# A planner that orders five engines: measured durations, a latency per engine, a port shared by two engines, and a transfer queue

## The chip, the cores and the metric

The kernel runs on one core of a Trainium2 chip. Its engines run their own instruction streams: TensorE (PE, with its weight loads PEld), VectorE (DVE), ScalarE (ACT), GpSimd (POOL), and SyncE (SP), which here only issues transfers. The metric is the device time of one launch in microseconds (us).

## The reference

Two blocks in a row, in float32: attention over a sliding window of 64 positions, and an expert-like layer ("SoLU" with a layer norm).

```python
# q, k, v: (8, 8, 576, 64); q and k are scaled by 6.12 beforehand
scores = q @ k.transpose(0, 1, 3, 2) / 8
scores = where((rel >= 0) & (rel < 64), scores, -1e9)      # rel = query - key
attn = exp(scores - max) / (sum + 1e-9)
x = (attn @ v) as 4608 tokens of 512
h = x @ w_in                                               # 512 x 1024
e = exp(h - max(h));  solu = h * e / (sum(e) + 1e-9)
ln = (solu - mean(solu)) / sqrt(var(solu) + 1e-6) * g_ln
out = ln @ w_out                                           # 1024 x 512
```

The weights w_in, w_out come as float64 and are brought to float32 on the chip by bit operations.

## The kernel before

The 4608 tokens are 36 tiles of 128. For each tile t the program does, in this order:

- **scores** (L375, PE): queries by keys into the PSUM tile pS. DVE (L390) takes the negative maximum of each of 8 heads (nmx) and moves the scores to SBUF (sS); ACT (L395) does the exponentials and their sums (sm); DVE (L408, L411) turns the sums into reciprocals (rec); POOL (L413) multiplies, one instruction for each head, 8 a tile.
- **transposes of the probabilities**: for tiles 0 to 4 on PE (L448) and copied to PT (L453). From tile 5 on ACT packs them by halves into a tile "raw" (L427), a transposing transfer on SP turns each half (L430), and DVE copies it to PT (L437), two copies a tile.
- **values** (L472, PE): V by PT into pO; ACT and DVE split the result into a high part xH (L486) and a rest xL (L487).
- **first matrix** (L515, PE): 24 matmuls of 128x512, three for each product (xH by the high weights, xH by their rest w, xL by the high weights) into pH. pH has one buffer of two banks: the next tile's L515 can't start before this tile's pH has been read.
- **norm**: DVE takes the maximum (L530, to a column of mst), ACT the exponential e (L532), DVE the product e·h and its sum (L535, the last reader of pH), then small columns on DVE (L538 to L546), ACT squares (L541), POOL takes the power −1/2 (L548), DVE a last product (L549), and POOL scales the two halves of e (L552).
- **transposes of e**: DVE packs each half (L578), a transfer turns it (L581), DVE unpacks it to y (L591), ACT and DVE split it into yH (L595) and yL (L597). The first three and last two tiles go through PE (L612).
- **second matrix** (L648, PE): 24 matmuls into pO, copied by ACT (L655) and stored by SP (L656).

The stages of several tiles overlap: scores run 3 or 4 tiles ahead of L515, and L648 two tiles behind it. From tile 6 on, tiles go in pairs: PE does the values of two tiles, the scores of two tiles, then L648, L515, L648, L515. In the first 66 us the weights are converted (L288 to L296) and split into a high part and a rest w (L312 to L319), and the first three tiles use plain float32 matmuls (L504, L636).

The order on each engine isn't written out. The code adds each piece of work to a `Plan` with an engine, a cost in ns, the tiles that it reads and writes, and a latency. `Plan.order` gives each piece a due time, counted back from the order in which PE's work was added, and then simulates the five engines: of the pieces that are ready on the engine that is free first, it takes the one due earliest. The instructions are emitted in the order that comes out, and on the chip each engine runs its own strictly in that order. SP is one of these engines, so a transfer that waits holds up those behind it. Pieces marked "loose" may leave the order in which they were added.

Of the kernel before, what the change touches and what calls it, by code (L numbers as in the profile page):

```python
# [57 lines left out]
class Plan:  # L58
# [4 lines left out]
    LATENCY = 150  # L63
# [6 lines left out]
    def op(self, engine, cost, emit, reads, writes, lat=0, loose=False):  # L70
        self.ops.append((engine, cost, emit, reads, writes, lat + self.LATENCY, loose))

    def dma(self, size, emit, reads, writes, loose=False):
        self.op("SP", max(350, size // (RATE if loose else 340)), emit, reads, writes, 2600, loose)

    def edges(self):
# [37 lines left out]
    def order(self):  # L114
# [31 lines left out]
        out = []  # L146
        while any(waiting.values()):
# [21 lines left out]
def tile_window_attention_solu_moe(  # L169
# [92 lines left out]
    def weight_block(i, src):  # L262
# [20 lines left out]
        for x in parts:  # L283
# [7 lines left out]
                tf()[:, x], tf()[:, x], EXP_LO, EXP_HI, ALU.max, ALU.min), [W], [W])  # L291
            plan.op("DVE", n // 3 * 2 + 18, lambda x=x: nc.vector.tensor_scalar(
                t()[:, x], t()[:, x], 0x07FFFFFF, 3, ALU.bitwise_and, ALU.logical_shift_left), [W], [W])
            plan.op("DVE", n + 170, lambda x=x: nc.vector.scalar_tensor_tensor(
                t()[:, x], hi()[:, x], -0x40000000, t()[:, x], ALU.bitwise_and, ALU.bitwise_or), [R, W], [W])
# [10 lines left out]
    def split(i):  # L306

        for x in range(2):
            reads = [("w", i), ("w", i, x), ("w", NC + 1 if i < NC else NW - 1)]
            last = reads[:2] + [("H", i, x)], [("w", NW + i, x)]  # L310
            if i < NC:
                plan.op("ACT", 600, lambda x=x: nc.scalar.copy(WH(i, x), W32(i)[:, x]), reads, [("H", i, x)])  # L312
                plan.op("DVE", 620, lambda x=x: nc.vector.tensor_sub(  # L313
                    WL(i)[:, x], W32(i)[:, x], WH(i, x).bitcast(F32)), *last)
# [4 lines left out]
            plan.op("DVE", 620, lambda x=x, f=f: nc.vector.scalar_tensor_tensor(  # L319
                WL(i)[:, x], W32(i)[:, x], g_sb[:, f:f + 1], WH(i, x).bitcast(F32), ALU.mult, ALU.subtract), *last)  # L320
# [39 lines left out]
    def scores(t):  # L360
# [22 lines left out]
    def softmax(t):
# [4 lines left out]
        for h in range(H):  # L388

            plan.op("DVE", 215, lambda h=h: nc.vector.tensor_tensor_reduce(  # L390
                SS(t)[:, h], PS(t)[:, h % 2, h // 2], mk, scale=-SCALE, scalar=BIG,
                op0=ALU.add, op1=ALU.min, accum_out=cols("nmx", h)),
                [("pS", t, h // 4)], [("sS", t, h), ("nmx", t, h)], lat=300)
        for h in range(H):
# [3 lines left out]
                [("nmx", t, h)], [("sS", t, h), ("sm", t, h)], lat=400)  # L398
# [6 lines left out]
        for o in range(0, H, n):  # L405
            s = slice(o, o + n)
            R = ("rec", t, o)
            plan.op("DVE", 160, lambda s=s: nc.vector.tensor_scalar_add(  # L408
                rec()[:, s], T("sm", t, [P, H], pool=st)[:, s], 1e-9),
                [("sm", t, h) for h in range(o, o + n)], [R])  # L410
            plan.op("DVE", 160, lambda s=s: nc.vector.reciprocal(rec()[:, s], rec()[:, s]), [], [R])  # L411
            for h in range(o, o + n):
                plan.op(engine, cost, lambda h=h: v.tensor_scalar(  # L413
                    SS(t)[:, h], SS(t)[:, h], rec()[:, h:h + 1], 0.0, ALU.mult, ALU.add),
                    [R], [("sS", t, h)])
# [18 lines left out]
    def transposes(t):
        if t >= CROSS_P:
            for x in range(2):
# [3 lines left out]
                    [("raw", NW + 2 * t, 2 + x)], [("PT", t, x)])  # L440
# [248 lines left out]
    def group(t):  # L689
        on(values, t + 1)  # L690
        if t != PAIRS:
            on(values, t + 2)
# [107 lines left out]
```

## Time and profile before

| | us |
|---|---|
| median of 3 runs (530.92 to 532.55) | 532.03 |
| the profiled execution | 531.16 |
| its span, first to last instruction | 529.4 |
| PE busy | 504.7 |
| DVE busy | 417.3 |
| ACT busy | 356.0 |
| POOL busy | 224.6 |

The granted TensorE clock is 0.999 over the span. PE's own records are pipelined: a matmul of 128x512 lasts 0.40 us in the records, while the next one starts after about 0.235. So a run of matmuls without gaps is recognised by the starts, not by the records' lengths. Of the transfers, SP issues 36 loads of queries and keys (qk, 640 KB), 36 of v (512 KB), 36 stores (256 KB) and 124 transposes; from issue to landing they take 5.3, 4.8, 2.7 and 3.2 us in the median.

### The profile page before, as it was taken

How to read it: one execution, taken by the hardware profiler on the slowest of the kernel's cores; microseconds unless marked ns; L12 is line 12 of the kernel's file. 1: busy time of each engine (PE TensorE's matmuls, PEld its weight loads, DVE VectorE, ACT ScalarE, POOL GpSimd, SP SyncE). 2: the span in 40 equal slices, each digit the busy share in tenths (PEclk: the TensorE clock that was granted, in tenths of full speed). 3: DMA queues.
4: the chain of work that ended last, by engine and by line, in shares of the span. 5: the costliest groups of instructions: out<-in, count | busy, mean ns of one | idle time of the engine just before them, and what ended most of it. 6: DMA issues, size and time to landing. Idle time of an engine off the chain costs nothing.

```text
span 529.4 us, 11654 instructions
## 1 busy us (share of the span) xinstructions
PE 504.7 (95%) x4072; PEld 392.2 (74%) x4072; DVE 417.3 (79%) x1327; ACT 356.0 (67%) x959; POOL 224.6 (42%) x406
## 2 busy tenths in 40 slices
PE   2779999999999999999999999999999999999996
PEld 2345577787888887787878787888788878787774
DVE  4979999888797878696978787978787878796631
ACT  4588776669586767777676768585858585855331
POOL 2056066444625460626261727272727272713220
PEclk9999999999999999999999999999999999999999
DMA  8994226887959798777789696969796959555201
GB/s 319 409 399 146 89 85 114 185 198 172 216 134 170 209 183 198 150 229 150 230 147 232 138 241 130 249 132 247 132 248 127 250 120 213 111 129 115 65 21 40
DMA packets 148507, 93.57 MB, mean 177 GB/s; under 512 B 132960, under 2 KB 132960, under 8 KB 148064
## 3 DMA queue, kind: packets, MB, share of 16 engines
q1 hardware_dynamic: 148448, 92.83, 72.1%
q8 instruction: 32, 0.52, 0.4%
q14 instruction: 27, 0.22, 0.1%
HBM read 50.86 MB, written 9.44 MB: 114 GB/s over the span
## 4 chain that ended last, share of the span: by engine, by line
PE 58%; DVE 17%; POOL 8%; DMA 8%; ACT 6%; issue 2%; ACTq 0%; POOLq 0%; DVEq 0%
PE pH L515 23%; PE pO L648 19%; DMA raw<-raw 7%; POOL sS L413 5%; PE pO L472 4%; PE pS L375 4%; PE pH L504 3%; DVE sS L390 3%; PE pO L636 3%; POOL e L552 3%; DVE y L591 3%; DVE e L535 2%; ACT sS L395 2%; DVE raw L578 2%; DVE mst L530 1%
## 5 line engine op out<-in xcount | busy, mean ns | idle before, releaser
L413 POOL TENSOR_SCALAR sS<-sS,rec 128x128 f32<-128x128 f32 x280 | 123.7, 460 | 50.7 <-DVE nmx L390 26.7
L395 ACT ACTIVATE sS<-sS,nmx 128x128 f32<-128x128 f32 x288 | 112.0, 392 | 10.5 <-DVE nmx L390 10.2
L648 PE MATMUL pO<-w_outH,yH 128*128 128x512 f32 x272 | 110.3, 405 | 0.0
L515 PE MATMUL pH<-w_inH,xH 128*128 128x512 f32 x264 | 106.3, 403 | 1.9 <-DVE mst L535 1.6
L648 PE MATMUL pO<-w,yH 128*128 128x512 f32 x272 | 108.1, 397 | 0.0
L548 POOL TENSOR_TENSOR mst<-mst,neghalf 128x1 f32<-128x1 f32 x36 | 28.2, 784 | 187.6 <-DVE mst L546 187.6
L648 PE MATMUL pO<-w_outH,yL 128*128 128x512 f32 x272 | 106.8, 393 | 0.0
L515 PE MATMUL pH<-w,xH 128*128 128x512 f32 x264 | 104.2, 398 | 0.0
L515 PE MATMUL pH<-w_inH,xL 128*128 128x512 f32 x264 | 103.6, 392 | 0.0
L552 POOL TENSOR_SCALAR e<-e,mst 128x512 f32<-128x512 f32 x72 | 69.5, 972 | 50.9 <-DVE mst L549 23.7
L427 ACT COPY raw<-sS 128x1024 uint16<-128x1024 uint16 x62 | 64.8, 1045 | 36.5 <-POOL sS L413 36.3
L515 PEld LDWEIGHTS pH<-w_inH,xH 128*128 128x128 f32 x264 | 49.5, 188 | 17.4 <-PE pO L648 4.3
L648 PEld LDWEIGHTS pO<-w_outH,yH 128*128 128x128 f32 x272 | 51.0, 187 | 15.0 <-issue 1.9
L648 PEld LDWEIGHTS pO<-w_outH,yL 128*128 128x128 f32 x272 | 51.1, 188 | 12.7
L541 ACT ACTIVATE sq<-e,mst 128x1024 bf16<-128x1024 f32 x36 | 41.4, 1151 | 27.1 <-DVE mst L538 22.7
L648 PEld LDWEIGHTS pO<-w,yH 128*128 128x128 f32 x272 | 51.1, 188 | 10.8
L530 DVE TENSOR_REDUCE mst<-pH 128x1 f32<-128x1024 f32 x36 | 43.8, 1216 | 19.5 <-PE pH L515 18.7
L578 DVE COPY raw<-e 128x1024 uint16<-128x1024 uint16 x62 | 45.2, 732 | 17.5 <-POOL e L552 17.5
L515 PEld LDWEIGHTS pH<-w_inH,xL 128*128 128x128 f32 x264 | 49.6, 188 | 12.6 <-DVE w L313 0.2
L515 PEld LDWEIGHTS pH<-w,xH 128*128 128x128 f32 x264 | 49.6, 188 | 11.3 <-issue 0.2
L591 DVE COPY y<-raw 128x1024 uint16<-128x1024 uint16 x62 | 48.6, 787 | 10.4 <-DMA raw<-raw 10.3
L390 DVE CUSTOM_DVE_ANT_0 sS<-pS,maskNone 128x128 f32<-128x128 f32 x224 | 53.5, 283 | 2.3 <-PE pS L375 1.9
(66 smaller groups left out, 743.6 us busy)
## 6 DMA issues: line engine op xcount, KB each, us to landing
qk<-qk SPq DMA_DIRECT2D x36, 640.0 KB, 5.3
v<-vS SPq DMA_DIRECT2D x36, 512.0 KB, 4.8
y<-ot SPq DMA_DIRECT2D x36, 256.0 KB, 2.7
raw<-w_out SPq DMA_DIRECT2D x4, 1024.0 KB, 11.8
raw<-w_in SPq DMA_DIRECT2D x3, 1024.0 KB, 11.9
raw<-raw SPq DMA_TRANSPOSE x124, 3.2
raw<-w_in SPq DMA_DIRECT2D x2, 512.0 KB, 6.6
g_sb<-gT SPq DMA_DIRECT2D x1, 4.0 KB, 14.3
```

Of the source, the lines that this page charges most:

```text
L390: plan.op("DVE", 215, lambda h=h: nc.vector.tensor_tensor_reduce(SS(t)[:, h], PS(t)[:, h % 2, h // 2], mk, scale=-SCALE, scalar=BIG, op0=A ...
L395: plan.op("ACT", 390, lambda h=h: nc.scalar.activation(SS(t)[:, h], SS(t)[:, h], AF.Exp, bias=cols("nmx", h), scale=-1.0, accum_out=cols(" ...
L413: plan.op(engine, cost, lambda h=h: v.tensor_scalar(SS(t)[:, h], SS(t)[:, h], rec()[:, h:h + 1], 0.0, ALU.mult, ALU.add), [R], [("sS", t, h)])
L427: plan.op("ACT", 1050, lambda x=x: nc.scalar.copy(XP(t)[:, x], SS(t)[:, 4 * x:4 * x + 4].bitcast(U16).rearrange("p h (n w) -> p w (h n)", ...
L515: plan.op("PE", 233, lambda n=n, c=c, x=x, w=w: nc.tensor.matmul(PH(t)[:, hs], x(t)[:, c], WH(c, h) if w is WH else WL(c)[:, h], start=(n ...
L530: plan.op("DVE", 1150, lambda: nc.vector.tensor_reduce(nmax(), PH(t), axis=AX.X, op=ALU.max, negate=True), [("pH", t)], [key(0)])
L541: plan.op("ACT", 1200, lambda: nc.scalar.activation(T("sq", t, [P, DFF], BF16), E(t), AF.Square, bias=nmean(), scale=1.0, accum_out=ss()), ...
L548: plan.op("POOL", 560, lambda: nc.gpsimd.tensor_tensor(kk(), kk(), neghalf, op=ALU.pow), [], [key(5)])
L552: plan.op("POOL", 770, lambda h=h, hs=hs: nc.gpsimd.tensor_scalar(E(t)[:, hs], E(t)[:, hs], nmean(), kk(), ALU.add, ALU.mult), [key(4), ke ...
L578: plan.op("DVE", 740, lambda h=h: nc.vector.tensor_copy(EP(t, h), E(t)[:, h * 512:(h + 1) * 512].bitcast(U16).rearrange("p (n w) -> p w n" ...
L591: plan.op("DVE", 740, lambda h=h: nc.vector.tensor_copy(Y(h).bitcast(U16).rearrange("p f (n w) -> p f w n", w=2), TP(t, h).rearrange("p w ...
L648: plan.op("PE", 233, lambda f=f, i=i, x=x, k=k, y=y, w=w: nc.tensor.matmul(PO(), y(t)[:, f], w(i, x), start=(f == k == 0), stop=(f == NF - ...
```

## The change

Only the planner's model and the costs handed to it change, and with them a few places where loads and groups are added. What is computed stays the same, instruction by instruction.

- One latency of 150 ns for all becomes a latency behind each engine (`AFTER`) plus one ahead of the engine that waits (`AHEAD_OF`). Between two pieces on one engine it is now 0 (90 before), except on SP.
- A piece may be marked as using the port that DVE and POOL share; the simulation then lengthens it where the other engine's marked piece still runs, by at most 120 ns on DVE and 500 on POOL.
- A transfer occupies SP for 550 ns only, and the transfer itself runs in a queue of its own; SP may run at most 6 us ahead of that queue. The transposing ones have 1300 instead of 1250.
- Costs are set anew (below, some of them).
- `group`, which adds a pair's values, scores, softmax and loads, takes lists of tiles; the loads of the second tile of a pair wait for the packing of its probabilities, as before. LEAD, PAD_S, PAD_P and PAD_E are 0 and have no effect.

```diff
-    LATENCY = 150
+    AFTER = {"PE": 220, "DVE": 40, "ACT": 40, "POOL": 40, "SP": 2400}
+    AHEAD_OF = {"PE": 110, "DVE": 0, "ACT": 0, "POOL": 100, "SP": 0}
...
+        def wait(j, i):
+            if self.ops[i][0] == self.ops[j][0] != "SP":
+                return 0
+            return self.ops[j][5] + self.AHEAD_OF[self.ops[i][0]]
...
-                due[j] = min(due[j], due[i] - (HASTE * (self.ops[j][1] + lat) if whole else 0))
+                due[j] = min(due[j], due[i] - (HASTE * (self.ops[j][8] + wait(j, i)) if whole else 0))
...
-            end = begin + self.ops[i][1]
-            free[e] = end
+            _, cost, _, _, _, _, _, shared, busy = self.ops[i]
+            if e in port and shared:
+                other = port["POOL" if e == "DVE" else "DVE"]
+                cost += max(0, min(other - begin, 120 if e == "DVE" else 500))
+                port[e] = begin + cost
+            free[e] = end = begin + cost
+            if e == "SP":
+                end = queue = max(begin, queue) + busy
+                free[e] = max(free[e], queue - 6000)
...
-        plan.op("DVE", 1150, lambda: nc.vector.tensor_reduce(
+        plan.op("DVE", 1225, lambda: nc.vector.tensor_reduce(
...
-            plan.op("DVE", 620, lambda h=h, hs=hs: nc.vector.tensor_sub(
+            plan.op("DVE", 690, lambda h=h, hs=hs: nc.vector.tensor_sub(
                 YL(t)[:, hs], Y(h), YH(t)[:, hs].bitcast(F32)),
-                [("y", t, h), ("yH", t, h)], [("yL", t, h)])
+                [("y", t, h), ("yH", t, h)], [("yL", t, h)], port=True)
...
+    def group(t, vs, ss, late=True):
+        vs = [u for u in vs if u < NTILE]
+        ss = [u for u in ss if u < NTILE]
+        for u in vs:
+            values(u)
+        for u in ss:
+            scores(u)
+        gate = [("gate", ss[-1])] if late and ss else []
+        on(load, ss[0] + 3, range(1)) if ss else None
+        on(load, vs[0] + 3, range(1, 2)) if vs else None
+        for u in ss:
+            softmax(u)
+            cross(u)
+        for u in ss[1:]:
+            on(load, u + 3, range(1), gate)
+        for u in vs[1:]:
+            on(load, u + 3, range(1, 2), gate)
```

Three places show what it moves. Names carry the tile's number first (rec_4 is tile 4's; the second number counts tiles of all kinds); line numbers of the changed kernel are about 20 higher.

DVE near 62 to 68 us, between the last weight block and tile 3's first matrix (w_8 to w_11 are the rests of w_in; rec_4 the reciprocals of tile 4), before:

```order
L487 TENSOR_TENSOR xL_3_656<-pO_39_606,xH_3_633 128x512
L313 TENSOR_TENSOR w_8_660<-w_0_145,w_inH_97 128x512 x2
L408 TENSOR_SCALAR rec_4_667<-sm_4_533 128x8
L313 TENSOR_TENSOR w_9_670<-w_1_187,w_inH_97 128x512 x2
L411 RECIPROCAL rec_4_667<-rec_4_667 128x8
L313 TENSOR_TENSOR w_10_677<-w_2_202,w_inH_97 128x512 x2
L538 TENSOR_SCALAR mst_1_465<-mst_1_465 128x1
L539 TENSOR_SCALAR mst_1_465<-mst_1_465 128x1
L313 TENSOR_TENSOR w_11_693<-w_3_255,w_inH_97 128x512
```

And now:

```order
L555 ISA mst_2_648 128x1
L333 TENSOR_TENSOR w_8_665<-w_0_149,w_inH_97 128x512 x2
L333 TENSOR_TENSOR w_9_678<-w_1_195,w_inH_97 128x512 x2
L333 TENSOR_TENSOR w_10_688<-w_2_206,w_inH_97 128x512 x2
L333 TENSOR_TENSOR w_11_693<-w_3_261,w_inH_97 128x512
L428 TENSOR_SCALAR rec_4_695<-sm_4_533 128x8
L431 RECIPROCAL rec_4_695<-rec_4_695 128x8
L558 TENSOR_SCALAR mst_1_467<-mst_1_467 128x1
```

The two steps of rec_4, which stood behind the second and the fourth of the copies, stand behind the seventh.

DVE near 142 to 146 us, where tile 8's first matrix ends and the values of tiles 9 and 10 begin (PT_10 is copied in two halves), before:

```order
L437 COPY PT_10_1595<-raw_28_1540 128x4x2x128
L549 TENSOR_TENSOR mst_7_1499<-mst_7_1499 128x1
L437 COPY PT_10_1595<-raw_28_1540 128x4x2x128
L578 COPY raw_23_1612<-e_7_1517 128x1024
L591 COPY y_6_1545<-raw_21_1466 128x4x2x128
L530 TENSOR_REDUCE mst_8_1650<-pH_8_1565 128x1
```

And now:

```order
L457 COPY PT_10_1599<-raw_28_1540 128x4x2x128
L617 TENSOR_TENSOR yL_6_1561<-y_6_1543,yH_6_1551 128x512
L457 COPY PT_9_1588<-raw_26_1527 128x4x2x128
L550 TENSOR_REDUCE mst_8_1612<-pH_8_1567 128x1
L457 COPY PT_10_1599<-raw_28_1540 128x4x2x128
L569 TENSOR_TENSOR mst_7_1498<-mst_7_1498 128x1
```

The second half of PT_10 has moved behind the maximum of tile 8, and the halves of tiles 9 and 10 alternate. The same holds for PT_12 and tile 10.

DVE in a pair of the later, regular part (the place where tile 24's norm ends and the reciprocals of tiles 27 and 28 come; sS_28 and nmx_28 are the last scores of tile 28), before:

```order
L390 ISA sS_28_4345,nmx_28_4346<-pS_28_4290,maskNone_90 128x128
L390 ISA nmx_28_4346 128x1
L549 TENSOR_TENSOR mst_24_4240<-mst_24_4240 128x1
L597 TENSOR_TENSOR yL_23_4384<-y_23_4360,yH_23_4372 128x512
L408 TENSOR_SCALAR rec_27_4403<-sm_27_4312 128x8
L411 RECIPROCAL rec_27_4403<-rec_27_4403 128x8
L578 COPY raw_57_4410<-e_24_4264 128x1024 x2
L408 TENSOR_SCALAR rec_28_4432<-sm_28_4382 128x8
L411 RECIPROCAL rec_28_4432<-rec_28_4432 128x8
L530 TENSOR_REDUCE mst_25_4446<-pH_25_4379 128x1
```

And now:

```order
L410 ISA sS_28_4366,nmx_28_4367<-pS_28_4289,maskNone_90 128x128
L410 ISA nmx_28_4367 128x1
L428 TENSOR_SCALAR rec_27_4393<-sm_27_4338 128x8
L431 RECIPROCAL rec_27_4393<-rec_27_4393 128x8
L598 COPY raw_57_4399<-e_24_4276 128x1024 x2
L611 COPY y_23_4334<-raw_55_4241 128x4x2x128
L428 TENSOR_SCALAR rec_28_4428<-sm_28_4388 128x8
L431 RECIPROCAL rec_28_4428<-rec_28_4428 128x8
L617 TENSOR_TENSOR yL_23_4353<-y_23_4334,yH_23_4344 128x512
L550 TENSOR_REDUCE mst_25_4447<-pH_25_4375 128x1
```

The last product of tile 24's norm (L549, now L569) has left these rows: it stands four scores of tile 28 further ahead. The second half of y_23 and its yL have moved behind the packing of e_24 and behind rec_28. On POOL, the 16 products behind it run as tiles 27, 28, 27, 28, four each, instead of 27 and 28, eight each; ACT packs the halves, and SP and DVE handle them, in that order.

More of the change, by code (lines that the diff above doesn't have):

```diff
@@ L43 @@
 PAIRS = 6
+LEAD = 0
 SPL = 3
 RATE = 240
+PADS = 12
+PAD_S = 0
+PAD_P = 0
+PAD_E = 0
 RINGS = {
@@ L68, in __init__, with op, dma @@
         self.ops = []
[L70 to L74, printed above, removed]
+    def op(self, engine, cost, emit, reads, writes, lat=0, loose=False, port=False, busy=None):
+        lat += self.AFTER[engine]
+        self.ops.append((engine, cost, emit, reads, writes, lat, loose, port or engine == "POOL", busy or cost))
+    def dma(self, size, emit, reads, writes, loose=False, rate=340):
+        self.op("SP", 550, emit, reads, writes, 0, loose, busy=max(350, size // rate))
     def edges(self):
@@ L146, in order @@
         out = []
+        queue, port = 0, {"DVE": 0, "POOL": 0}
         while any(waiting.values()):
@@ L318, in split @@
                     reads + [("g",)], [("H", i, x)])
-            plan.op("DVE", 620, lambda x=x, f=f: nc.vector.scalar_tensor_tensor(
-                WL(i)[:, x], W32(i)[:, x], g_sb[:, f:f + 1], WH(i, x).bitcast(F32), ALU.mult, ALU.subtract), *last)
+            plan.op("DVE", 690, lambda x=x, f=f: nc.vector.scalar_tensor_tensor(
+                WL(i)[:, x], W32(i)[:, x], g_sb[:, f:f + 1], WH(i, x).bitcast(F32), ALU.mult, ALU.subtract), *last, port=True)
     def QK(t):
@@ L397, in softmax @@
                 accum_out=cols("sm", h)),
[L398 removed]
+                [("nmx", t, h)], [("sS", t, h), ("sm", t, h)], lat=185)
         def rec():
@@ L439, in transposes @@
                     XP(t)[:, 2 + x].rearrange("p w (h n) -> p h w n", h=4)),
-                    [("raw", NW + 2 * t, 2 + x)], [("PT", t, x)])
+                    [("raw", NW + 2 * t, 2 + x)], [("PT", t, x)], port=True)
             return
@@ new lines, in moe_norm @@
+        plan.op("DVE", 1225, lambda: nc.vector.tensor_tensor_reduce(
+            E(t), PH(t), E(t), scale=1.0, scalar=0.0, op0=ALU.mult, op1=ALU.add, accum_out=sp()),
+            [("pH", t)], H2 + [key(2)], lat=80)
+        plan.op("DVE", 70, lambda: nc.vector.tensor_scalar_mul(nmean(), sp(), -1.0 / DFF), [key(2)], [key(4)])
+        plan.op("DVE", 70, lambda: nc.vector.tensor_scalar_add(se(), se(), 1e-9), [], [key(1)])
+        plan.op("DVE", 100, lambda: nc.vector.reciprocal(se(), se()), [], [key(1)])
@@ L688, in tile_window_attention_solu_moe @@
     prep(7)
[L689 to L692, printed above, removed]
-        both = t + AHEAD, t + AHEAD + 1
-        for u in both:
-            on(scores, u)
-        if t == PAIRS:
-            on(load, t + AHEAD + 2, range(1))
-        on(load, t + AHEAD + 3, range(1))
-        on(load, t + AHEAD + 1, range(1, 2))
-        for u in both:
-            on(softmax, u)
-            on(cross, u)
-        on(load, t + AHEAD + 4, range(1), [("gate", t + AHEAD + 1)])
-        if t != PAIRS:
-            on(load, t + AHEAD + 2, range(1, 2), [("gate", t + AHEAD + 1)])
+    def group(t, vs, ss, late=True):
[15 more added lines that the diff above has]
+            on(load, u + 3, range(1, 2), gate)
     for t in range(NTILE + BEHIND):
@@ L710, in tile_window_attention_solu_moe @@
         if t == PAIRS - 1:
+            on(load, t + AHEAD + 2, range(1))
+        if t == PAIRS:
             on(load, t + AHEAD + 2, range(1))
@@ L740, in tile_window_attention_solu_moe @@
                 attend(t)
+            elif t == PAIRS:
+                group(t, [t + 1], [t + AHEAD, t + AHEAD + 1], False)
             elif t == PAIRS + 1:
-                on(values, t + 1)
-                on(load, t + AHEAD + 1, range(1, 2))
+                group(t, [t + 1], [t + AHEAD + 1, t + AHEAD + 2][:LEAD], False)
             elif even:
-                group(t)
+                group(t, [t + 1, t + 2], [t + AHEAD + LEAD, t + AHEAD + LEAD + 1])
             if t - BEHIND == PLAIN_OUT:
```

81 lines of the change are left out of this document (37 added, 44 removed).

## The prediction

> **What bounds the kernel now.** I read the busy shares first, then the stretches by stage, then who waited for whom on PE, then single stretches of the timeline.
>
> ```profile
> span 529.4 us, 11654 instructions
> PE 504.7 (95%) x4072; PEld 392.2 (74%) x4072; DVE 417.3 (79%) x1327; ACT 356.0 (67%) x959; POOL 224.6 (42%) x406
> ```
>
> PE is busy for 95% of the span, so only its gaps can be won. The stretches show where they are; each row after the first one runs from the start of one pair of "values" groups (L472) to the next, that is two tiles.
>
> ```profile
> core 0: us, PE busy (x) PEld busy (x) DVE busy (x) ACT busy (x) POOL busy (x), PEclk, DMA share, GB/s
> 52.90:66.20 13.30, 13.30 (x100) 7.43 (x98) 13.13 (x20) 10.30 (x21) 0.55 (x1) 1.00 0.28 89
> 197.00:224.70 27.70, 27.04 (x225) 21.63 (x224) 21.40 (x71) 19.27 (x52) 10.60 (x22) 1.00 0.82 183
> 251.30:279.60 28.30, 27.07 (x227) 21.63 (x226) 23.56 (x75) 19.05 (x53) 13.71 (x24) 1.00 0.81 193
> 279.60:306.70 27.10, 26.76 (x225) 21.54 (x224) 21.33 (x71) 19.18 (x52) 11.27 (x22) 1.00 0.84 177
> 306.70:333.70 27.00, 26.89 (x227) 21.58 (x226) 22.52 (x74) 19.05 (x52) 13.78 (x23) 1.00 0.83 191
> 333.70:360.30 26.60, 26.60 (x227) 21.63 (x226) 21.94 (x72) 19.07 (x52) 13.55 (x23) 1.00 0.80 194
> 413.50:440.50 27.00, 26.79 (x226) 21.53 (x225) 22.32 (x74) 19.05 (x52) 13.08 (x23) 1.00 0.86 188
> 440.50:467.50 27.00, 26.85 (x227) 21.57 (x226) 21.90 (x72) 19.06 (x52) 13.15 (x23) 1.00 0.79 168
> ```
>
> A pair without any wait takes 26.60 us (333.70:360.30). Of the eleven pairs between 170.4 and 467.5 the six others shown here are longer, by 1.1, 1.7, 0.5, 0.4, 0.4 and 0.4: together **4.5 us**, and this is all that a better order can win there. Two engines end these waits:
>
> ```profile
> PE pH L515 <- DVE mst L535: 1.6, 4, 0.8
> PE pO L472 <- DVE PT L437: 0.8, 2, 0.4
> ```
>
> First, L515 waits until L535 has read the one bank pair pH; second, L472 waits for the copy PT of the transposed probabilities. (The idle times are smaller than the loss, since a matmul's record lasts past the start of the next.) Before 66 us the second limit rules: DVE is busy 13.13 of 13.30 us, with the splitting of the weights.
>
> **The change part by part.** No instruction is added or removed. On PE the order is the old one except for two groups of scores before 45 us (S1 and S3), which are split or joined. What changes is the order on DVE, ACT, POOL and SP.
>
> **Part 1, tile 4's softmax (loss).** T4, the transposes L448 of tile 4, stands in PE's order between the two halves of tile 3's L515. It needs the eight products L413 on POOL, and these need rec_4.
>
> ```profile
> 62.71 1.31 DVE L313 TENSOR_TENSOR w<-w,w_inH 128x512 fp32r<-128x512 f32 x2
> 65.26 0.20 DVE L411 RECIPROCAL rec<-rec 128x8 f32<-128x8 f32 x1
> 66.71 0.69 DVE L313 TENSOR_TENSOR w<-w,w_inH 128x512 fp32r<-128x512 f32 x1
> 29.49 2.79 POOL L413 TENSOR_SCALAR sS<-sS,rec 128x128 f32<-128x128 f32 x8 [24.86 <-DVE nmx L390]
> 65.65 4.51 POOL L413 TENSOR_SCALAR sS<-sS,rec 128x128 f32<-128x128 f32 x8 [15.22 <-DVE rec L411]
> 69.05 1.49 PE L448 MATMUL pS<-ident,sS 128*128 128x128 f32 x8
> 70.29 0.48 PE L515 MATMUL pH<-w_inH,xH 128*128 128x512 f32 x1
> ```
>
> Now rec_4 ends at 65.46 and POOL runs 65.65 to 70.16; PE goes on at 70.29, so POOL already sets this point. In the new order rec_4 stands behind the seventh copy L313, which now ends at 67.40. DVE is also behind in its work: when L535 of tile 1 starts, one L292, one L294 and two rows of scores that used to precede it are still to do.
>
> ```profile
> 48.59 0.70 PE L504 MATMUL pH<-w,xH 128*128 128x512 f32 x1 [0.28 <-DVE mst L535]
> L294 DVE SCALAR_TENSOR_TENSOR w<-raw,w 128x1024 int32<-128x1024 int32 x7 | 8.5, 1218 | 0.0
> L292 DVE TENSOR_SCALAR w<-w 128x1024 int32<-128x1024 int32 x7 | 5.3, 759 | 0.1
> ```
>
> The two alone are 1.22 + 0.76 = 2.0 us, with the scores some 2.2. I take 1.3 of it back, because L535 of tile 1 itself comes earlier by about that: the scores of tile 4, which it follows, wait for less on POOL (PE's L504 waits for it at 48.59, so PE gains there for a while). Net 0.9, with 0 and 2.2 as ends. Less 0.3 for rec_4 and the small columns that no longer stand ahead: the seventh copy ends at 68.0, rec_4 at 68.4. The eight products then have one weight copy beside them instead of four; between 2.79 (none) and 4.51 (four) I take 3.2. They end near 71.7, and PE goes on near 71.8 instead of 70.29: **+1.5 us**. Ends: 67.75 + 2.79 gives +0.3; 68.9 + 4.51 gives 73.4 and +3.1. Behind it PE runs dense, so nothing returns what is lost here, and what PE won at 48.59 is waited off in front of T4.
>
> A row on the shared port bears on this.
>
> ```profile
> 71.98 1.12 DVE L319 SCALAR_TENSOR_TENSOR w<-w,g_sb,w_outH 128x512 fp32r<-128x512 f32 x1
> 73.09 0.72 DVE L319 SCALAR_TENSOR_TENSOR w<-w,g_sb,w_outH 128x512 fp32r<-128x512 f32 x1
> ```
>
> The same copy takes 0.40 longer beside POOL's work, more than the 120 ns that the new table allows DVE. [...]
>
> **Part 2, values of tiles 10 and 12 (loss).** In the new order the second copy PT_10 (and PT_12) stands behind L530 of tile 8 (10). L530 can't start before PE has finished L515, just when L472 begins.
>
> ```profile
> L437 DVE COPY PT<-raw 128x1024 uint16<-128x1024 uint16 x62 | 47.1, 767 | 8.3 <-DMA raw<-raw 8.2
> 360.38 1.23 DVE L530 TENSOR_REDUCE mst<-pH 128x1 f32<-128x1024 f32 x1 [0.92 <-PE pH L515]
> 361.52 0.68 DVE L578 COPY raw<-e 128x1024 uint16<-128x1024 uint16 x1
> 251.29 1.62 PE L472 MATMUL pO<-PT,v 128*64 128x64 f32 x48
> 253.32 0.69 PE L472 MATMUL pO<-PT,v 128*64 128x64 f32 x16 [0.42 <-DVE PT L437]
> ```
>
> The last two rows show such a wait: three quarters of a pair's values run, then the last quarter waits for its PT. It is due some 1.5 after the start (the record of the three quarters lasts 1.62, and a record outlasts the start of the next by about 0.1). Seen from the start of the values (360.3, where the stretch 333.70:360.30 ends), L530 frees DVE at 361.52, that is after 1.22, and the copy takes 0.77: 1.99. So 0.5 is lost, twice: **+1.0 us**. The order is strict, so the lower end, 0, needs PE to be late for another reason.
>
> **Part 3, L535 of tile 11 (small loss).** It now stands behind L530, yL, y and PT.
>
> ```profile
> L591 DVE COPY y<-raw 128x1024 uint16<-128x1024 uint16 x62 | 48.6, 787 | 10.4 <-DMA raw<-raw 10.3
> ```
>
> With 1.23 for L530 and for L535, 0.69 for yL (the shape of the copy at 66.71), 0.79 and 0.77, that is 4.7 us of the 5.6 that PE spends on one L648 group (24 matmuls at about 0.235), less what PT waits for its transposes. I take +0.2, ends 0 and +1.0.
>
> **Part 4, the pairs from tile 13 on (gain).**
>
> ```profile
> 344.24 0.15 DVE L549 TENSOR_TENSOR mst<-mst 128x1 f32<-128x1 f32 x1
> 344.56 2.51 POOL L552 TENSOR_SCALAR e<-e,mst 128x512 f32<-128x512 f32 x2 [2.14 <-ACT yH L595]
> 347.06 7.07 POOL L413 TENSOR_SCALAR sS<-sS,rec 128x128 f32<-128x128 f32 x16
> 349.13 1.22 DVE L530 TENSOR_REDUCE mst<-pH 128x1 f32<-128x1024 f32 x1 [0.91 <-PE pH L515]
> 350.42 1.05 ACT L427 COPY raw<-sS 128x1024 uint16<-128x1024 uint16 x1 [0.34 <-POOL sS L413]
> 351.38 1.11 ACT L532 ACTIVATE e<-pH,mst 128x1024 f32<-128x1024 f32 x1
> 352.61 1.23 DVE L535 CUSTOM_DVE_ANT_0 e<-pH,e 128x1024 f32<-128x1024 f32 x1 [0.77 <-ACT e L532]
> 354.56 0.40 PE L515 MATMUL pH<-w_inH,xH 128*128 128x512 f32 x1
> ```
>
> This is the chain behind pH: L549 on DVE lets POOL scale e, then POOL does the products, ACT copies them (L427), and only then does ACT run L532, which L535 needs. L535 ends at 353.84 and PE needs it at 354.56: 0.7 us of room even in a good pair. The new order puts one copy L591 (0.79) and four rows of scores behind L549, which ran ahead of it; other work takes part of their place, so I count the copy alone, 0.8. L532 can follow no earlier than L530's end (349.13 + 1.22 = 350.35), and from 351.38 it has 1.0 to come forward, so the 0.8 passes whole and the room grows to 1.5. The longest single wait, in the pair 251.30:279.60 with 1.7 for two waits, is about 1.0, so most vanish. I take 3.6 of the 4.5 (80%) as gone; ends 2.2 (half) and 4.5. On SP the second transposes of e now follow the load of qk two tiles on, which waits for L375 in the same pair: L375 ends as the second L578 does, so that costs nothing; if the load were late, these transposes would be too, by as much.
>
> **Sum.** +1.5 + 1.0 + 0.2 − 3.6 = **−0.9 us**. The profiled execution took 531.16 us (span 529.4 and 1.8 around it), so 530.3 by its own clock; the median shown, 532.03, is 0.87 above it, so I forecast **531.1**. The ends add up to −4.2 and +2.9.
>
> **The rivals.** *Faster:* part 1 costs only its low end, since the products run at 2.79 and DVE has no backlog, and all of the 4.5 goes: 0.3 + 1.0 − 4.5 = −3.2, 528.8. For it: POOL alone does reach 2.79. Against it: DVE is 99% busy in 52.90:66.20, so a backlog stays. *Slower:* POOL now does the products of a pair as halves in turn (27, 28, 27, 28), so the first tile's second half is third and its PT may reach L472 late in every disturbed pair. A wait like the one at 253.32 costs 253.32 − 252.79 = 0.5; in six pairs of eleven, as many as wait now, +3.2, so −0.9 + 3.2 = +2.3, 534.3. It decides once that half's transposes land over 1.5 us later than now; the earlier start of POOL speaks against it. *Nothing:* the orders off PE only move idle time about, no wait goes or comes: 532.0.
>
> **How the numbers follow.** About 0.3% (1.6 us) is what a measurement of this kernel can tell from no change, so "same" is 530.4 to 533.6. The forecast has 0.42 and the nothing rival 0.10, both within it: same 0.52. The faster rival has 0.30, the slower 0.18. The range reaches from a little under the faster rival's time, 528.6, to the upper end of the sum, 532.03 + 2.9, so 535.0.
>
> **What would show it.** Right: PE's second half of tile 3's L515 resumes 1 to 2 us late behind T4; two waits of L472 for PT near 145 and 173 us; pairs of 26.6 us from about 200 on. Wrong: T4 no later than 70.5, or pairs after 200 still at 27 or more. A wait of L472 for PT in many pairs would be the slower rival. What I have not seen in any row is how the transfers meet in the new order; that would make the prediction wrong first.

## The result

The changed kernel takes **535.72 us** (median of 5 runs, 535.22 to 538.01) against 530.92 of the kernel before (5 runs beside them): ratio 1.0088, 95% interval 1.0064 to 1.0111. It is slower by 0.9%; 531.1 was forecast, with 535.0 as the upper end.

The page of the profiled execution (538.01 us), with busy times and the clock by slices:

```profile
span 536.2 us, 11656 instructions
...
PE 510.7 (95%) x4072; PEld 396.3 (74%) x4072; DVE 426.7 (80%) x1327; ACT 354.8 (66%) x959; POOL 242.2 (45%) x406
...
PEclk9969979999999999999999999999999999999999
```

The last row is new: in the third and the sixth of 40 slices PE got less than its full clock. The other four runs have spans of 533.4 to 534.2 at mean clocks of 0.990 to 0.993. The stretches of the same execution, cut where the clock changes, and then by pairs of tiles from one start of the values to the next:

```profile
core 0: us, PE busy (x) PEld busy (x) DVE busy (x) ACT busy (x) POOL busy (x), PEclk, DMA share, GB/s
27.11:30.52 3.41, 1.42 (x4) 0.70 (x5) 3.34 (x17) 1.41 (x8) 0.93 (x3) 1.00 1.02 413
30.52:40.76 10.24, 8.51 (x46) 4.92 (x45) 5.40 (x18) 8.25 (x22) 5.06 (x14) 0.50 0.91 355
71.48:74.89 3.41, 1.66 (x5) 0.51 (x3) 3.31 (x16) 2.51 (x5) 1.26 (x3) 1.00 0.07 26
74.89:81.72 6.83, 5.99 (x18) 4.32 (x18) 5.08 (x25) 4.58 (x19) 6.46 (x15) 0.50 0.02 5
153.05:180.28 27.23, 26.82 (x225) 21.71 (x224) 22.51 (x73) 18.96 (x52) 14.33 (x23) 1.00 0.73 148
180.28:208.60 28.32, 26.84 (x225) 21.71 (x224) 24.28 (x75) 19.07 (x52) 16.66 (x24) 1.00 0.89 199
208.60:235.20 26.60, 26.60 (x225) 21.63 (x224) 22.54 (x72) 19.07 (x52) 12.04 (x22) 1.00 0.81 176
```

Twice the clock is exactly half, for 10.24 and 6.83 us: three and two times 3.41. In the 3.41 us ahead of each PE is busy for less than half, 1.42 and 1.66. In the pairs the forecast gain is there in full: from 208.60 on each takes 26.60 (the first of them is shown); the two before them are longer by 0.63 and 1.72. The waits of PE, in us, times and the longest one:

```profile
PE pH L524 <- DVE w L316: 4.6, 3, 2.5
PE pS L468 <- ACT PT L473: 1.6, 2, 0.8
PE pO L492 <- DVE PT L457: 1.5, 1, 1.5
PE pS L468 <- POOL sS L433: 0.9, 1, 0.9
```

And the timeline of the head, where the time went (start, us, engine, line):

```profile
29.11 2.42 PE L524 MATMUL pH<-w,xH 128*128 128x512 f32 x4 [2.46 <-DVE w L316]
37.29 4.12 PE L524 MATMUL pH<-w,xH 128*128 128x512 f32 x5
73.18 0.50 PE L535 MATMUL pH<-w,xH 128*128 128x512 f32 x1 [0.82 <-DVE w L333]
74.60 1.52 PE L468 MATMUL pS<-ident,sS 128*128 128x128 f32 x4 [0.92 <-POOL sS L433]
76.94 1.11 PE L468 MATMUL pS<-ident,sS 128*128 128x128 f32 x4 [0.82 <-ACT PT L473]
77.70 0.77 PE L535 MATMUL pH<-w_inH,xH 128*128 128x512 f32 x1
...
73.24 0.20 DVE L431 RECIPROCAL rec<-rec 128x8 f32<-128x8 f32 x1
73.63 3.89 POOL L433 TENSOR_SCALAR sS<-sS,rec 128x128 f32<-128x128 f32 x8 [21.68 <-DVE mst L559]
...
76.21 0.58 ACT L473 COPY PT<-pS 128x512 f32<-128x512 f32 x1
```

T4 starts at 74.60 (69.05 before) and tile 3's second half of L535 at 77.70 (70.29). It stops for POOL, as predicted, and a second time for ACT's copy of PT_4's first half. From 37.29 five L524 last 4.12 us, 0.82 each; before, ten from 35.64 last 4.56:

```profile
35.64 4.56 PE L504 MATMUL pH<-w,xH 128*128 128x512 f32 x10
```

So two things are new besides the late rec_4: a wait that was not there before, and a slow PE. The experiments ask what each costs.

The second wait comes from the order in which the plan writes the engines' work into one list, not from ACT's own order. Before, both halves of T4 were written ahead of that copy; now the copy stands between them, and the second half, which writes the same PSUM tile, waits for its reader. PE's instructions with their waits, before and after:

```
L448 pS_76<-ident,sS_4 [waits PE,Pool]
L448 pS_76<-ident,sS_4 [waits Pool] x7

L468 pS_76<-ident,sS_4 [waits PE,Pool]
L468 pS_76<-ident,sS_4 [waits Pool] x3
L468 pS_76<-ident,sS_4 [waits Activation,Pool]
L468 pS_76<-ident,sS_4 [waits Pool] x3
```

### The profile page after: what moved, and what is told of

It reads as the page before. It is cut to its first block, busy times and chain, and to the rows that moved or that the text cites. A ratio compares the mean times of both kernels' runs of the same rounds, so it can differ in the third digit from the quotient of the medians.

```text
span 536.2 us, 11656 instructions
## 1 busy us (share of the span) xinstructions
PE 510.7 (95%) x4072; PEld 396.3 (74%) x4072; DVE 426.7 (80%) x1327; ACT 354.8 (66%) x959; POOL 242.2 (45%) x406
## 4 chain that ended last, share of the span: by engine, by line
PE 83%; DVE 10%; ACT 4%; DMA 2%; issue 1%; POOL 0%; ACTq 0%; POOLq 0%; DVEq 0%
PE pO L668 33%; PE pH L535 32%; PE pO L492 6%; PE pS L395 6%; PE pH L524 3%; ACT sS L415 1%; DVE w L316 1%; PE pO L656 1%; DVE w L314 1%; DVE mst L550 1%; DMA raw<-raw 1%; ACT e L552 1%; DVE w L333 1%; DVE sS L410 1%; PE pS L632 1%
## 5 line engine op out<-in xcount | busy, mean ns | idle before, releaser
L433 POOL TENSOR_SCALAR sS<-sS,rec 128x128 f32<-128x128 f32 x280 | 140.1, 519 | 57.4 <-DVE nmx L410 25.0
L568 POOL TENSOR_TENSOR mst<-mst,neghalf 128x1 f32<-128x1 f32 x36 | 26.0, 723 | 192.9 <-DVE mst L566 192.9
L535 PE MATMUL pH<-w_inH,xH 128*128 128x512 f32 x264 | 106.8, 405 | 0.0
L535 PE MATMUL pH<-w,xH 128*128 128x512 f32 x264 | 105.0, 400 | 0.8 <-DVE w L333 0.8
L535 PE MATMUL pH<-w_inH,xL 128*128 128x512 f32 x264 | 104.6, 396 | 0.0
L572 POOL TENSOR_SCALAR e<-e,mst 128x512 f32<-128x512 f32 x72 | 72.9, 1019 | 27.9 <-DVE mst L569 19.1
L506 ACT CAST xH<-pO 128x512 fp32r<-128x512 f32 x33 | 19.2, 585 | 66.6 <-PE pO L492 66.6
L535 PEld LDWEIGHTS pH<-w_inH,xH 128*128 128x128 f32 x264 | 50.1, 190 | 13.6 <-issue 0.5
L535 PEld LDWEIGHTS pH<-w,xH 128*128 128x128 f32 x264 | 49.9, 189 | 13.2 <-DVE w L333 1.6
L535 PEld LDWEIGHTS pH<-w_inH,xL 128*128 128x128 f32 x264 | 50.2, 190 | 12.7 <-issue 0.2
L550 DVE TENSOR_REDUCE mst<-pH 128x1 f32<-128x1024 f32 x36 | 44.0, 1222 | 18.9 <-PE pH L535 18.0
L410 DVE CUSTOM_DVE_ANT_0 sS<-pS,maskNone 128x128 f32<-128x128 f32 x224 | 52.2, 285 | 4.1 <-PE pS L395 4.1
L415 ACT ACTIVATION_READ_ACCUMULATOR sS<-sS,nmx 128x1 f32 x288 | 54.3, 188 | 0.0
```

What stands on the lines that cost most here:

```text
L410: plan.op("DVE", 211, lambda h=h: nc.vector.tensor_tensor_reduce(SS(t)[:, h], PS(t)[:, h % 2, h // 2], mk, scale=-SCALE, scalar=BIG, op0=A ...
L415: plan.op("ACT", 390, lambda h=h: nc.scalar.activation(SS(t)[:, h], SS(t)[:, h], AF.Exp, bias=cols("nmx", h), scale=-1.0, accum_out=cols(" ...
L433: plan.op(engine, cost, lambda h=h: v.tensor_scalar(SS(t)[:, h], SS(t)[:, h], rec()[:, h:h + 1], 0.0, ALU.mult, ALU.add), [R], [("sS", t, ...
L535: plan.op("PE", 235, lambda n=n, c=c, x=x, w=w: nc.tensor.matmul(PH(t)[:, hs], x(t)[:, c], WH(c, h) if w is WH else WL(c)[:, h], start=(n ...
L550: plan.op("DVE", 1225, lambda: nc.vector.tensor_reduce(nmax(), PH(t), axis=AX.X, op=ALU.max, negate=True), [("pH", t)], [key(0)])
L568: plan.op("POOL", 560, lambda: nc.gpsimd.tensor_tensor(kk(), kk(), neghalf, op=ALU.pow), [], [key(5)])
```

## The experiments

Two theories: **clock** (PE's idle time in the head halves its clock, and that is most of the loss) and **waits** (PE is late because DVE, POOL and ACT are late; the slow clock falls on time that PE would wait anyway). Line numbers shift a little from kernel to kernel.

**Spare matmuls in front of w3's block.** Tile 0's first product is started over in an idle 2.5 us; the result is the same.

```diff
-    plan.op("PE", 860, lambda ...: matmul(PH half x, XH c, W32(c) half x))
+    for k in (0, 1, 2, c) if (t, c, x) == (0, 3, 0) else (c,): matmul(PH half x, XH k, W32(k) half x)
```

> The kernel after, with three extra matmuls (blocks 0, 1 and 2 of tile 0's first product, half 0, computed a second time from the start) put in front of block 3, where PE idles 2.7 us for w3. They fill an idle time and move nothing else. Clock theory (the half clock from 30.5 to 40.8 us comes from PE's low busy share in the 3.4 us before, and costs more than the wait): no granted clock under 0.9 between 30 and 41 us, OUT of tile 0 starts at 60 to 61.5 instead of 62.4, time 1 to 3 us under after's 535.7. Waits theory (the half clock is only a by-product, PE waits for DVE anyway): the clock may stay up, but OUT of tile 0 at 62.4 +-0.4 and the time 535.7 +-0.7.

534.3 us, 1.0056 (1.0038 to 1.0073): 1.4 under the changed kernel, within the 1 to 3 of the clock theory. The half clock between 30 and 41 us is gone and the second matrix of tile 0 starts at 59.70 instead of 62.38. But an earlier stretch came, and the one near 74 stayed:

```profile
15.82:19.23 3.41, 1.66 (x19) 0.75 (x18) 3.34 (x4) 0.26 (x1) 0.00 (x0) 1.00 1.02 423
19.23:22.65 3.42, 3.42 (x7) 1.49 (x6) 3.35 (x7) 0.00 (x0) 0.00 (x0) 0.50 1.02 402
```

Here the first 3.41 us hold an earlier wait for weights. The drops lie elsewhere than in after: at 19.23 and 73.85 here, at 30.52 and 74.89 there.

**Nine more spare matmuls** around the last matmul of tile 3's first half, into the bank that the second half overwrites.

```diff
+    if (t, h, n) == (3, 0, 11): spare(4)   # ahead of the matmul
+    if (t, h, n) == (3, 0, 11): spare(5)   # behind it
```

> As the run before, and nine more matmuls of 0.235 us whose result is overwritten, four in front of the last matmul of the first half of tile 3's L535 and five behind it, where PE idles for the weight copy and for tile 4's products. Clock theory: neither half-clock stretch is left, the time is 3 to 6 us under after's 535.7 (529.7 to 532.7), and tile 3's second half runs at 0.235 a matmul. Waits theory: both stretches may vanish, but the time stays within 1 us of 535.7, since PE's start behind tile 4's products is set by POOL and ACT.

532.48 us, 1.0027 (1.0004 to 1.0050): 3.2 gained, as the clock theory has it, though not every run is free of the half clock. The 12 runs settle the price, since the program is one and the same: five have a clock of 0.999 or 1.0 and spans of 529.3 to 529.4; two 0.997 and 530.6 to 530.7; four 0.994 and 532.4 to 532.7; one 0.990 and 533.9. One window of 3.41 us at half clock lowers the mean by 3.41 / 2 / 529 = 0.003, so these are 0, 1, 2 and 3 windows, and each costs about **1.5 us** here. (The runs of the changed kernel itself with two and five windows lie 4.1 and 6.9 above 529.3, so 2.0 and 1.4 a window.) The profiled run has none:

```profile
70.69 1.29 PE L468 MATMUL pS<-ident,sS 128*128 128x128 f32 x4
72.91 0.52 PE L468 MATMUL pS<-ident,sS 128*128 128x128 f32 x3 [0.92 <-ACT PT L473]
73.59 0.33 PE L468 MATMUL pS<-ident,sS 128*128 128x128 f32 x1 [0.17 <-POOL sS L433]
73.68 0.48 PE L542 MATMUL pH<-w_inH,xH 128*128 128x512 f32 x1
```

This is the order of after without the clock: T4 1.64 us later than before, tile 3's second half 3.39 later. It is POOL's last product that releases PE at the end. The waits theory, no more than 1 us of gain, falls; the waits that it names are the rest of the loss in the head.

**rec_4 alone** put back ahead of the third weight copy, as in the kernel before.

> The kernel after, with rec_4 alone moved back ahead of the third weight copy L333, as in the kernel before. If tile 4's late products are the cause of the second loss: T4 starts about 74 instead of 74.6 (POOL needs 4.5 beside the copies instead of 3.9), the gain is 0.5 to 1.5 us by the waits alone. Clock theory: more only if the half clock at 74.9 goes as well, then 3 to 4 us. If rec_4 does not matter because the weight copies themselves are late: within 0.5 us of 535.7.

534.48 us, 1.0060 (1.0043 to 1.0078): by the medians a gain of 1.2, within the 0.5 to 1.5 of the waits alone, though the interval overlaps that of after. T4 starts at 69.95 and not near 74 as expected, since the stretch near 30 us did not come in this profile. But its second half still stands behind ACT's copy, and the clock drops at 71.68:

```profile
69.95 0.49 PE L482 MATMUL pS<-ident,sS 128*128 128x128 f32 x3
70.71 0.33 PE L482 MATMUL pS<-ident,sS 128*128 128x128 f32 x1 [0.27 <-POOL sS L447]
73.06 1.09 PE L482 MATMUL pS<-ident,sS 128*128 128x128 f32 x4 [2.02 <-ACT PT L487]
73.80 0.78 PE L549 MATMUL pH<-w_inH,xH 128*128 128x512 f32 x1
```

**T4 in one piece alone**: the list is written so that the copy and ACT's next entry follow T4's second half. No engine's order changes.

```diff
+    moved = [at("ACT", ("PT", 4, 0)), at("ACT", ("sS", 5, 4))]
+    out = [i for i in out if i not in moved]
+    n = out.index(at("PE", ("pS", 76, 1))) + 1
+    out[n:n] = moved
```

> The kernel after, with the order on every engine unchanged; only in the merged list the copy of the first half of PT_4 (and ACT's next entry behind it) is written behind the second half of T4 instead of between the halves, so that this second half no longer gets a wait for ACT. Theory that this added wait is a term of its own: T4 runs in one piece of eight as in before, tile 3's second half of L535 resumes 1.0 to 1.5 us earlier relative to T4's start than in after (3.1 us behind it), and the time is 1 to 2 us under 535.7. Rival, that POOL's products set it anyway: T4's second half waits for POOL instead, gain under 0.4.

535.82 us, 1.0078 (1.0047 to 1.0108): no gain, the rival was right. The last product now holds PE, and tile 3's second half comes 3.1 us behind T4's start as in after:

```profile
74.33 2.56 PE L477 MATMUL pS<-ident,sS 128*128 128x128 f32 x7 [0.93 <-POOL sS L442]
77.30 0.48 PE L477 MATMUL pS<-ident,sS 128*128 128x128 f32 x1 [0.42 <-POOL sS L442]
77.43 0.77 PE L544 MATMUL pH<-w_inH,xH 128*128 128x512 f32 x1
```

Each of the two waits hides behind the other. So **both together**:

> The edit of the run before, and rec_4 ahead of the third weight copy. If the head's second loss is these two (rec_4 and the wait for the copy): T4 starts at about 70 in one piece, tile 3's second half at 71.5 to 72, tile 4's L535 at 84 to 85 instead of 92.05; no or a shorter half-clock stretch near 72; time 530 to 532.5. If the half clock is set by PE idling for w3 alone: a stretch stays and the time is 533 or more.

532.90 us, 1.0027 (1.0006 to 1.0047), 0.4 above the upper end. In the profile tile 3's second half follows T4's start (72.44) after 2.22, but half-clock windows at 18.82 and 35.89 made the part ahead of it late. **Both, and spare matmuls** in front of blocks 1 and 3 of tile 0 (five, in the way of the first experiment):

> The kernel after in its own order, with rec_4 ahead of the third weight copy, T4 unsplit, and the five spare matmuls in front of blocks 1 and 3 of tile 0. If rec_4, the split and the half clock are the whole loss of the head: runs without a half-clock stretch have a span of 527 to 528 (529.3 of the run with the nine spare matmuls, less 1.3 to 2.3 for T4), T4 goes on in one piece, tile 3's second half at 71.3 to 72.3, tile 4's L535 at 84 to 85; median 529 to 530. If something else is lost in the head: undisturbed runs stay at 529 or more.

530.97 us, 1.0003 (0.9986 to 1.0021). Tile 3's second half starts at 72.46. Only two of 12 runs have a clock of 0.999 or 1.0, with spans of 528.2 and 528.4, little above the 527 to 528 expected; the median misses 529 to 530, and in the profiled run a window near T4 still drops:

```profile
68.76:72.17 3.41, 2.25 (x9) 1.07 (x8) 3.31 (x19) 2.63 (x9) 3.41 (x7) 1.00 0.01 2
72.17:75.59 3.42, 3.41 (x9) 2.59 (x9) 3.35 (x17) 3.19 (x14) 1.51 (x4) 0.50 0.02 5
```

**The head of before, the rest of after.** The first 566 entries of the list are those of before, the others keep after's order.

```diff
+    first = set(FIRST)   # 566 numbers
+    out = FIRST + [i for i in out if i not in first]
```

> The first 566 of the plan's 4010 entries (to the start of tile 5's L535, about 100 us) in the order of before, the rest in the order of after. If the loss sits in the head's order alone and the gain in the pairs alone: OUT of tile 1 at 78 and tile 4's L535 at 82.8 as in before, no half clock, pairs of 26.6 us, the two waits of the values of tiles 10 and 12 (2.3 us) still there; time 530.9 - 4.5 + 2.3 = 528.7 (527.7 to 529.7). If the late part needs the head of after, or the loss is elsewhere too: 531 or more.

529.75 us, **0.9962** (0.9940 to 0.9985). The six runs with a clock of 0.998 or more have spans of 527.0 to 527.3, which with 1.8 around them are 528.8 to 529.1 for 528.7 expected; the six at 0.995 to 0.997 have 528.6 to 528.9, and with them the median is just above the 527.7 to 529.7 expected. The loss sits in the head, the gain behind it. **The same, with spare matmuls** in front of blocks 1 and 3:

> The head in the order of before (566 entries), the rest of after, and spare matmuls that repeat finished blocks of tile 0's first product: two in front of block 1, three in front of block 3. Clock theory: a 3.41 us window stays over about 0.54 busy there more often, so fewer runs than 6 of 12 show a half-clock stretch and the median goes from 529.75 to 528.8 to 529.3; runs without one stay at a span of 527.0 to 527.3. If the spare matmuls delay PE: every run 0.5 to 1 us longer than 527.1.

528.99 us, **0.9956** (0.9934 to 0.9978), the fastest of all: nine of 10 runs have 0.998 or more (eight of them spans of 526.9 to 527.3), as the clock theory expected. Its 0.54 is 1.84 of 3.41 us, the window from 28.32 on that kept the clock in the run before (last section). In these nine the spare matmuls delay nothing; the one run at 0.997, which is the profiled one, has 529.9, 1.0 more than the slowest of the run before. Ten and twelve runs are few, and the intervals of the two overlap, so that the spare matmuls help here too is likely, not shown. Its first two pairs:

```profile
147.81:175.02 27.21, 26.80 (x225) 21.69 (x224) 22.81 (x74) 19.22 (x52) 14.64 (x24) 1.00 0.69 143
175.02:202.32 27.30, 26.83 (x225) 21.71 (x224) 23.24 (x74) 18.93 (x52) 14.61 (x23) 1.00 0.89 200
```

**The head of before, three spare matmuls in front of block 3, and the second copies PT_10 and PT_12 moved ahead**, to win the two waits of the values.

```diff
+    move PT_10's second copy ahead of the maximum L550 of tile 8
+    move PT_12's second copy ahead of the last copies L598 of tile 9
```

> The head in the order of before (first 566 entries), the rest in the order of after, the three spare matmuls in front of w3's block, and on DVE the second copies PT_10 and PT_12 moved ahead of L550 of tile 8 and ahead of the last copy L598 of tile 9. If the two waits of the values cost 2.2 as in the run with the head alone: pairs 7 to 8 and 9 to 10 go from 27.2 and 28.2 to 26.6, span 525 where no clock stretch falls (527.0 there), 526.8 by the median. If DVE's later L550 gives it back: within 0.5 of 528.8.

531.13 us, 0.9989 (0.9967 to 1.0012): neither of the two answers expected, and worse than without the moves; runs at a clock of 1.0 have spans of 528.1 to 529.3 instead of 527. The moved copy of PT_10 waits on DVE for its transfer, and L550 (here L600) with all that follows it waits behind that copy; PE waits elsewhere:

```profile
147.43 0.75 DVE L503 COPY PT<-raw 128x1024 uint16<-128x1024 uint16 x1 [1.22 <-DMA raw<-raw]
148.07 1.21 DVE L600 TENSOR_REDUCE mst<-pH 128x1 f32<-128x1024 f32 x1
...
152.44 0.50 PE L718 MATMUL pO<-w_outH,yH 128*128 128x512 f32 x1 [1.62 <-DVE xL L553]
```

**The parts of the change, each taken back alone**: the port, the queue, the latencies, the durations.

> The kernel after without one part of the change: the plan no longer lengthens DVE's and POOL's work for the shared port. It puts the first copy of PT_4 behind three exponentials of tile 5 instead of four and PT_12 ahead of L550 of tile 10, but leaves rec_4 behind the seventh weight copy. If the port's model is what spoils the head: 531 to 533. If it is the common effect of latencies and durations (rec_4 stays late): 534 to 536, with V12's wait of 1.7 gone.

> The kernel after without the transfer queue in the plan (SP's cost of a load as in before, no backlog). The head's order on DVE is that of after up to the first 160 entries, rec_4 and the split T4 included, so the head's loss stays: 534 to 537 if the pairs stay at 26.6. If the queue is what keeps the pairs free of waits, as the port did: 540 or more.

> The kernel after with one latency for all engines again (150 ns, and the old longer ones of the sums), port, queue and durations left. T4's copy stands behind three exponentials and PT_10 and PT_12 ahead of L550, rec_4 still late. If the latencies are what loses the head: 530 to 533. If they are what frees the pairs: 536 or more, with waits of L535 in the pairs.

> The kernel after with the durations of DVE, PE and ACT of before put back into the plan, latencies, port and queue left as they are. rec_4 stays behind the seventh weight copy, PT_10 and PT_12 stand ahead of L550 again. If the durations carry the order of the head: 531 to 533. If they hardly matter: 533 to 536, less the 2.3 of the two values.

| taken back | us | ratio to before |
|---|---|---|
| port | 548.37 | 1.0302 (1.0263 to 1.0341) |
| queue | 534.47 | 1.0053 (1.0034 to 1.0072) |
| latencies | 540.69 | 1.0159 (1.0126 to 1.0192) |
| durations | 535.58 | 1.0067 (1.0041 to 1.0094) |

The port and the latencies carry the free pairs. For the port this was neither of the answers expected. For the latencies the time was one of the two, but the waits of L535 that were expected with it did not come, except for one. Without the port in the plan PE waits again for the readers of pH and pO (first two rows); with the old latencies the values wait for PT (last row), by 0.4 to 0.5 in four of the later pairs:

```profile
PE pH L535 <- DVE mst L555: 5.4, 6, 2.5
PE pO L668 <- DVE xL L507: 3.1, 3, 1.6
...
PE pO L492 <- DVE PT L457: 5.9, 6, 2.4
```

No part taken back alone gives a head without loss: rec_4 stays behind the seventh copy in all four.

## Why the prediction was wrong

**The step that failed** is the sum. It counts each idle time of PE once, as a wait, and gives every matmul behind it its duration of before; the clock stands in no term. In after the clock is also at half for 10.24 and 6.83 us, behind 3.41 us in which PE worked 1.42 and 1.66; with spare matmuls in these gaps the profile shows 1.00 in both places, and a window at half clock cost some 1.5 us. Three of the five runs of after stand at a clock of 0.990, that is three windows, 4.6 us by the runs of the same order with spare matmuls (533.9 against 529.3). The sentence behind part 1, "Behind it PE runs dense, so nothing returns what is lost here", holds for the waits alone: without a half-clock window PE is 3.39 late behind T4 and 3.42 late at the last values ahead of the pairs. In the profile of after it is 9.25 late there. The three rows are of the kernel before, of the run with the nine spare matmuls, and of after:

```profile
131.29 1.15 PE L472 MATMUL pO<-PT,v 128*64 128x64 f32 x32
134.71 1.15 PE L492 MATMUL pO<-PT,v 128*64 128x64 f32 x32
140.54 1.15 PE L492 MATMUL pO<-PT,v 128*64 128x64 f32 x32
```

Without a window the order of after takes 529.3 + 1.8 = 531.1, the very number forecast. This is luck for a good part, since two terms miss in opposite directions: the head loses 3.4 and not 1.5, the pairs win 4.5 and not 3.6. The terms:

- **Part 1** (+1.5, ends +0.3 and +3.1) was sized too small even without the clock. The path is the one forecast: rec_4, the eight products, and PE goes on when the last of them is done. But it goes on at 73.68, 3.39 later than before and above the upper end. In the undisturbed run the weight copies begin at 64.47 instead of 62.71, rec_4 ends at 69.45 where 68.4 was forecast, and the products take 3.89 where 3.2 was taken:

```profile
64.47 4.67 DVE L333 TENSOR_TENSOR w<-w,w_inH 128x512 fp32r<-128x512 f32 x7
69.25 0.20 DVE L431 RECIPROCAL rec<-rec 128x8 f32<-128x8 f32 x1
69.65 3.89 POOL L433 TENSOR_SCALAR sS<-sS,rec 128x128 f32<-128x128 f32 x8 [21.70 <-DVE mst L574]
```

  Of DVE's backlog 1.3 was taken back because L535 of tile 1 would come that much earlier; it came 0.7 earlier (46.62 against 47.30), and L535 of tile 2, right ahead of the copies, 2.4 later (63.33 against 60.96). The upper end was too low by its own terms as well: with the full 2.2 of backlog the products start near 69.8 and not at 68.9, and 4.51 for them gives +4.0. The wait for ACT's copy, which stood in PE's list of waits, was overlooked, but behind a late rec_4 it costs nothing, as T4 in one piece shows. It costs once rec_4 is early: by the medians 534.48 with the split and 532.90 without it. Taking back both brings the undisturbed span from 529.3 to 528.3, not to the 527.1 of the head of before. In the profile of that run (both taken back, five spare matmuls) rec_4 ends at 66.57 instead of 65.46, the products take 5.51 instead of 4.51 beside five weight copies in a row, and PE goes on at 72.46 instead of 70.29; further this was not taken apart.
- **"What PE won at 48.59 is waited off in front of T4."** In the undisturbed run tile 0's second matrix starts 0.9 earlier than before (58.39 against 59.29), so the win exists. But PE also came sooner to w3's block and waited 2.46 there (29.11) instead of 1.6:

```profile
PE pH L504 <- DVE w L296: 2.8, 2, 1.6
```

  The wait costs nothing by itself, since the block comes at 28.93 and 29.11, yet the 3.41 us around it hold 1.42 us of work instead of 1.85 (last section), and in after the clock is 0.50 from 30.52 on.
- **Part 2** (+1.0, no upper end above it). Both waits came where named, with 0.63 and 1.72, so +2.35 in the profile of after. In the other profiles that keep the order of these two places the first is 0.6 to 0.8 and the second 0.6 to 1.8; why the second varies is open.
- **Part 3** (+0.2). No wait of L535 for the column is left: 0.
- **Part 4** (−3.6, ends −2.2 and −4.5). All of the 4.5 went, the full end.
- **The rivals.** "Slower" put the price in late halves of PT in six pairs; no pair from 208.60 on has one. The time near its 534.3 came from elsewhere. A wait of its kind does come with the old latencies, in four of the later pairs, at 0.4 to 0.5. "Faster" was right that all of the 4.5 goes, and wrong on part 1.

The 3.2 for the products was taken with one weight copy beside them, between 2.79 with none and 4.51 with four; the measured 3.89 is above it. In the profile of after two further weight copies (L339) follow from 76.55 on, before the products end at 77.52, so 3.89 does not give the time beside one copy. That DVE and POOL share a port is an assumption of the plan. The rows show only that the times differ: 2.79, 3.89 and 4.51 for the eight products, and 0.72 and 1.12 for the copy L319, the longer one beside POOL's L552 (71.05, 1.51 long).

## What to carry to other kernels

Where PE runs at its full clock in the profile of before, an edit that bunches its idle time can cost more than the wait: behind the 2.46 us at 29.11 the clock was at half for 10.24 us. So look at how long PE works in each 3.41 us, not only at the length of the waits: here 1.42 us of work stood ahead of that drop, and in the kernel before 1.85 us kept the full clock. When a plan merges several engines' work into one list, compare the waits of the instructions as well as each engine's order: an engine can get a new wait although its order is the old one. And take a large reordering apart by its stretches: here the head of one order and the rest of the other are faster than both.

## What the hardware showed

In the profiles of the kernel before and of after the clock is at half in the last 0.73 and 0.49 us of the span, behind 3.41 us without work on PE. Ahead of that the stretches at half clock have one, two or three times 3.41 us: 3.42 from 24.90 on in the run with the head of before, 6.83 from 71.68 on with rec_4 alone, 10.24 from 30.52 on in after. With the head of before and spare matmuls the drop is at 25.87. The kernel before has lower clocks too, in some executions: its mean clock is 0.997 or less in 5 of the 23 runs beside the first experiments and in 13 of 24 beside later ones; the profiled one has 0.999. A window here is 3.41 us, counted in such steps from a drop. The last 3.41 us ahead of a drop, and one that was kept, in the run with the head of before:

```profile
21.49:24.90 3.41, 1.74 (x22) 1.12 (x21) 3.40 (x19) 2.96 (x10) 0.00 (x0) 1.00 1.03 398
24.90:28.32 3.42, 3.42 (x23) 1.40 (x25) 1.82 (x2) 2.01 (x11) 0.00 (x0) 0.50 1.03 413
28.32:31.73 3.41, 1.84 (x23) 1.03 (x19) 2.73 (x16) 1.47 (x7) 0.67 (x2) 1.00 1.02 410
```

And one kept in the kernel before, around its wait for w3, 147 windows ahead of the drop at 528.63:

```profile
26.87:30.28 3.41, 1.85 (x23) 0.93 (x16) 2.85 (x18) 1.71 (x10) 0.79 (x3) 1.00 1.02 414
```

Of the windows read here, with PE's work in us, the full clock was lost behind 0.97 (port taken back), 1.42 and 1.66 (after), 1.66 and 1.81 (first spare matmuls), 1.66 (rec_4 alone), 1.74 (the head of before, without and with spare matmuls) and 2.25 (both taken back, five spare matmuls). It was kept behind 1.76 (rec_4 alone), 1.84 (first spare matmuls, and head of before), 1.85 (before), 1.92 (after) and 1.99, 2.14 and 2.29 (nine more spare matmuls). The two overlap, so no limit is shown. In the 2.25 much of the work is transposes on PE; without these it is 0.75. Whether transposes count less is not shown either: the 2.29 have 0.95 beside theirs and kept the clock.

In after three windows at half clock were followed by another:

```profile
30.52:33.93 3.41, 2.64 (x10) 1.54 (x8) 1.72 (x7) 2.99 (x11) 1.86 (x6) 0.50 1.03 409
33.93:37.35 3.42, 2.46 (x35) 1.93 (x33) 1.94 (x7) 2.20 (x9) 0.00 (x0) 0.50 1.02 411
74.89:78.30 3.41, 2.57 (x10) 1.67 (x10) 3.10 (x19) 3.41 (x18) 3.41 (x8) 0.50 0.02 5
```

A stretch ended behind 3.04 us of work (73.85:77.26, first spare matmuls) and behind 3.41 and 3.42 (37.35:40.76 and 78.30:81.72 in after). In each of the three windows above PE has a wait: 0.77 ahead of 33.14, 0.96 ahead of 36.24, 0.82 ahead of 76.94.
